# A transformer block on one core: the first token group's evictions, dense groups and norms in another order

## The chip, the cores and the metric

The kernel runs on one core of a Trainium2 chip. A core has five engines with instruction queues of their own: TensorE (PE; it loads weights and multiplies into the accumulator banks of PSUM), VectorE (DVE), ScalarE (ACT), GpSimd (POOL) and SyncE (SP, which here issues every DMA). Each queue runs strictly in order, and engines wait for each other on semaphores. The metric is the time of one execution on the device in microseconds. Three runs of the kernel before took 260.52 us in the median (260.51 to 261.05).

## The reference

One adaptive-norm transformer block over 2048 tokens of 512 features, in bfloat16. A vector `c` gives six rows of modulation; then an attention in a sliding window of 256 keys with 32 heads of 16, and then an MLP across the tokens:

```python
mod = (_silu(c) @ w_mod).reshape(c.shape[0], 6, 1, -1)      # sa, ca, ga, sb, cb, gb
h = _layernorm(x) * (1 + ca) + sa
qkv = (h @ wqkv)                                            # 32 heads of 16
scores = q k^T * 16 ** -0.5, masked to 0 <= i - j < 256
x = x + ga * ((softmax(scores) @ v) @ wo)
h = _layernorm(x) * (1 + cb) + sb
u = gelu(einsum('bsd,sf->bdf', _layernorm(h), w1) + b1)     # sums over tokens
x = x + gb * (einsum('bdf,fs->bds', u, w2) + b2).T
```

## The kernel before

The 2048 tokens are four token groups of 512 (`tg` 0 to 3), each of four tiles of 128. The attention works through units `u`: in a token group, four groups of eight heads (`g8`), and in each of these five kinds `k`, so 20 units per token group, with the place `ul = 5 * g8 + k`. A unit has score products on PE (into two tiles `pss` of a pool of three, each of two banks), two exponentials on ACT (`et`, L614, halves a = 0 and 1), and products with V (into `po`, the one bank of the attention's products). Kinds 0 and 1 are the even heads, kind 2 is the far corner of the window for both, kinds 3 and 4 are the odd heads. In token group 0, kinds 0 and 3 have four score products with narrow exponentials (512 columns), kinds 1 and 4 twelve with wide ones (1024), kind 2 thirty-two with wide ones.

All else on PE is a dense group: 16 products of 512 columns, or 8 transpositions, into the single bank `dn`, which VectorE evicts before the next may begin. Dense groups are V of a tile (`v_group`, L283), q or k of eight heads (`qk_group`, L306), the transpositions of the normed tokens (`transpose_group`, L252), the modulation rows (`bc_group`, L336, which reads eight loads of `wmod` and sends its result through DRAM into `bc`), the biases (`bias_group`, L359) and wo. One unit takes at most one dense group.

The order is written out by the program itself. In the loop from L912, unit u issues: the first exponential, the scores of unit u + 1, then (if unit u - 1 is of kind 2 or 4) the products of u - 1, the dense group, the second exponential, the eviction of the group, and otherwise only now the products of u - 1. `plan` (L778) says with `lay(ul, group)` at which place of the token group each dense group stands. Groups of the next token group (its first q, k and two V tiles, its transpositions) are laid into the end of the one before. Before unit 0 there are V of tile 0 (through `po`) and of tile 1 (through `dn`).

Work of VectorE and GpSimd that isn't bound to a place stands in chains: lists of steps with costs. `fill` puts a step into VectorE's queue where the planner's own clocks (`clock`, in us) say that the engine has time; a chain whose step gave GpSimd work goes on only when the planner's clock of GpSimd says so. The first norm of the next token group is such a chain: statistics on VectorE (`ln1_stats`, L228), for every second tile a reciprocal root on GpSimd, and `ln1_apply` (L240), which for later token groups is 2 GpSimd instructions per tile. GpSimd also makes the even and odd copies of q (L330) and the quotient of the attention (`merge`, L683). `fold_wod` (L826) multiplies wo by a row of `bc`, also on GpSimd.

SyncE's queue in token group 0, in order, after the first inputs: at unit 0 two copies of V (`copy_vc`, L649, of tiles 0 and 1 into `Vc`), then a load of x, two fills of `Vc` with zeros, and x, `wmod`, `wo` in pieces "paced" behind exponentials, with two more copies of V each at units 3, 4 and 5. The copies of a group of heads are read by the products of its kinds 2 and 4.

After unit 79 the MLP follows, with TensorE alone as its tight engine.

Of the kernel before, what the change touches and what calls it, by code (L numbers as in the profile page):

```python
# [20 lines left out]
ND = D // P  # L21
# [9 lines left out]
def kernel(  # L31
# [327 lines left out]
    def bias_group(pool):  # L359
        def mms():  # L360
            pb = pool.tile([P, NF + NT], DT.bfloat16, name="dn")
            nc.tensor.transpose(pb[:], b12[:], identity[0 : NF + NT, 0 : NF + NT])
            return pb

        def evac(pb):
            nc.vector.tensor_copy(out=bFM[:], in_=pb[:])
        return mms, evac, 0.2
# [37 lines left out]
    with tc.manual_schedule():  # L405
# [372 lines left out]
        def plan(tg):  # L778
            at, then = {}, {}

            def lay(ul, group):
                assert ul not in at, (tg, ul)
                at[ul] = group

            def qk(ul, g, g8, kind):
                lay(ul, qk_group(g, g8, kind, ps_dn))

            for n in (2, 3):
                lay(n - 2, v_group(tg, n, ps_dn))
            if tg == 0:  # L790
                for ul, g8, kind in ((2, 1, "q"), (3, 1, "k"), (4, 2, "q"), (5, 2, "k"), (6, 3, "q"), (7, 3, "k")):
                    qk(ul, tg, g8, kind)
                lay(8, bias_group(ps_dn))
                lay(13, bc_group(ps_dn))
                then[18] = [(lambda g=g: fold_wod(g), 0.0) for g in range(ND)]
            else:
                if tg == 1:
                    order = ((2, 1, "k"), (3, 2, "q"), (4, 2, "k"), (5, 3, "q"), (8, 3, "k"))
                else:
                    order = ((2, 2, "k"), (3, 3, "q"), (4, 3, "k"))  # L800
                for ul, g8, kind in order:
                    qk(ul, tg, g8, kind)
                for ul, fc, k in {2: ((8, 10, 0), (10, 11, 0)), 3: ((8, 13, 0), (10, 12, 0), (11, 12, 1))}.get(tg, ()):
                    lay(ul, part_group(fc, k))
                for ul in (6, 7, 9, 10) if tg == 1 else (5, 6, 7, 9):
                    tb = next(wo_next)
                    lay(ul, wo_group(tb, ps_dn))
                    then[ul] = ln23(tb)
            if tg + 1 < NG:
                t0, t1, q0, v0, k0, q1, v1 = (10, 11, 12, 16, 14, 15, 18) if tg == 0 else (11, 12, 13, 14, 15, 17, 16)  # L810
                lay(t0, transpose_group(tg + 1, 0, ps_dn))
                lay(t1, transpose_group(tg + 1, 1, ps_dn))
                lay(v0, v_group(tg + 1, 0, ps_dn))
                lay(v1, v_group(tg + 1, 1, ps_dn))
                for ul, g8, kind in ((q0, 0, "q"), (k0, 0, "k"), (q1, 1, "q")):
                    qk(ul, tg + 1, g8, kind)
                if tg:
                    qk(18, tg + 1, 1, "k")
                    qk(19, tg + 1, 2, "q")
            else:  # L820
                for n, fc in enumerate((6, 7, 8, 9)):
                    for k in range(2):
                        lay(12 + 2 * n + k, part_group(fc, k))
            return at, then
# [6 lines left out]
        def at_unit(tg, ul, u, behind):  # L831
            if ul == 0 and tg + 1 < NG:
                st = lambda g, t0=0: [
                    (lambda tl=tl: ln1_stats(g, tl), 0.8, lambda tl=tl: 4 * g + tl in loaded) for tl in range(t0, 4)
                ]

                def ap(tl):
                    ln1_apply(tg + 1, tl)
                    return 1.13
                add_chain((st(1) if tg == 0 else []) + [(lambda tl=tl: ap(tl), 0.0) for tl in range(4)], first=True)  # L840
                if tg == 0:
                    add_chain(st(2) + st(3))
            if tg == 0 and ul == 6:
                nc.vector.memset(mod_add[:], 0.0)
                nc.vector.memset(mod_add[32:64, :], 1.0)
                nc.vector.tensor_copy(out=sT_rep[:], in_=sT[:].unsqueeze(2).to_broadcast([P, ND, 32]))
                clock["dve"] += 0.42
            if tg == 0 and ul % 5 == 3:
                ones_of_v(1, ul // 5, ul // 5 + 1)
                clock["act"] += 0.5  # L850
            if tg == 0 and ul == 1:
                for half in range(2):
                    part64 = slice(64 - 64 * half, 128 - 64 * half)
                    dma.dma_start(
                        out=Vc[half][part64, :, 8:H, :],
                        in_=zero[part64, :].rearrange("p (h d) -> p h d", d=2 * DH)
                        .unsqueeze(1).to_broadcast([64, 4, H - 8, 2 * DH]),
                    )
            if tg == 0 and 2 <= ul < 6:
                loaded.update((4 + 2 * ul, 5 + 2 * ul))  # L860
            if ul in (3, 4, 5) or (tg < 2 and ul == 0):
                copies_for(tg, max(ul - 2, 0))
            if 0 < tg < NG - 1 and ul == 17:
                copies_for(tg + 1, 0)
            while q_loads and ul != 3:
                load_q(*q_loads.pop(0))
            if tg == 0 and ul < 4:
                pair = slice(8 + 2 * ul, 10 + 2 * ul)
                paced(xall[:, pair, :], x_rows[:, pair, :], behind)
            if tg == 0 and 2 <= ul < 10:  # L870
                v, js = (2, 4, 3, 5)[ul // 2 - 1], slice(ul % 2 * 2, ul % 2 * 2 + 2)
                paced(wmod[:, js, v * D : (v + 1) * D], w_mod_v[:, js, v * D : (v + 1) * D], behind)
            if tg == 0 and 10 <= ul < 12:
                js = slice(ul % 2 * 2, ul % 2 * 2 + 2)
                paced(wod[:, js, :], wo_v[:, js, :], behind)
            if tg == 1 and ul == 2:
                modw.release()
                w1box["pool"] = tc.alloc_tile_pool(name="w1pool", bufs=1, side="right")
                w1box["a"] = w1box["pool"].tile([P, NA, F], DT.bfloat16, name="w1a")
                w1box["v"] = B_w1.rearrange("(sc p) f -> p sc f", p=P)  # L880
                w1box["sc"] = iter([(sc, n) for sc in range(NA) for n in range(2)])

            for sc, n in [x for x in [next(w1box.get("sc", iter(())), None)] if x]:
                part_f = slice(n * F // 2, (n + 1) * F // 2)
                paced(w1box["a"][:, sc, part_f], w1box["v"][:, sc, part_f], behind)
# [19 lines left out]
                on_pool(for_pool)  # L905

        emit_scores(0)
        mms, evac, _ = v_group(0, 1, ps_dn)
        evac(mms())
        clock.update(pe=1.3, dve=2.4, dn=1.4)  # L910
        ready = {0: (0.5, 0.5)}
        for u, (tg, g8, k) in enumerate(units):  # L912
            ul = 5 * g8 + k
            if ul == 0:
                at, then = plan(tg)
            half = 0.5 if (tg, k) in ((0, 0), (0, 3)) else 0.92
            behind = emit_exp(u, 0)
            before = clock["act"]
            clock["act"] = max(clock["act"], ready[u][0]) + half
            if u + 1 < len(units):  # L920
                emit_scores(u + 1)
                if units[u + 1][2] == 2:
                    first = max(clock["pe"], before) + 0.3
                    clock["pe"] = max(first, clock["act"] + 0.05) + 0.42
                else:
                    first = clock["pe"] = max(clock["pe"], clock["act"] - 0.1) + 0.4
                ready[u + 1] = (first + 0.1, clock["pe"] + 0.1)
            closes = u > 0 and units[u - 1][2] in (2, 4)
            if closes:
                products(u - 1)  # L930
            group = at.get(ul)
            if group:
                tile_ = group[0]()
                clock["pe"] = max(clock["pe"], clock["dn"]) + (0.55 if group[2] > 1 else 0.2 if group[2] == 0.2 else 0.9)
            emit_exp(u, 1)
            clock["act"] = max(clock["act"], ready[u][1]) + half
            if group:
                fill(clock["pe"] + 0.05)
                evacuate(group, tile_)
                if ul in then:  # L940
                    add_chain(then[ul])
            if u > 0 and not closes:
                products(u - 1)
            fill(clock["pe"])
            at_unit(tg, ul, u, behind)
        u += 1
        emit_av(u - 1)
# [206 lines left out]
```

## Time and profile before

| what | value |
| --- | --- |
| median of 3 runs | 260.52 us |
| the profiled execution | 259.97 us, its span 258.2 us |
| PE busy | 238.8 us, 92% of the span |
| ACT busy | 164.7 us, 64% (nearly all of it before 166 us) |
| DVE busy | 171.3 us, 66% |
| POOL busy | 120.7 us, 47% |
| attention, token group 0 | 13.9 to about 50 us |
| MLP | from about 166 us to the end |

A line of a timeline gives the start and length in us, the engine and line, what is written and read, and how many such instructions are merged; in brackets the idle time of the engine just before and what ended it. Line numbers are those of the kernel before.

### The profile page before, as it was taken

What the parts mean: (1) busy time and instruction counts of PE and PEld (TensorE: products, weight loads), DVE (VectorE), ACT (ScalarE), POOL (GpSimd) and SP (SyncE); (2) the same over time, 40 slices, a digit from 0 to 9 for tenths busy, and PEclk for the clock granted to TensorE, in tenths of its full rate; (3) what the DMA queues carried; (4) which work ended last, traced back from release to release, by engine and by line L of the source; (5) the groups of instructions that cost most, each with busy time, mean ns of one, the idle gap of its engine ahead of it and who ended that gap; (6) DMA issues with size and microseconds to landing.
All of it is one profiled execution on the core that took longest, in us unless ns stands there. A gap on an engine that the chain in (4) does not pass through costs nothing.

```text
span 258.2 us, 11273 instructions
## 1 busy us (share of the span) xinstructions
PE 238.8 (92%) x4993; PEld 129.5 (50%) x4993; DVE 171.3 (66%) x361; ACT 164.7 (64%) x193; POOL 120.7 (47%) x206
## 2 busy tenths in 40 slices
PE   6988879899989999999999999999999999999994
PEld 2534445455555565555555555544444444444444
DVE  6678878875788888888777897589703112432454
ACT  6588998999999999999999999500055220000000
POOL 6103963689367998887655699664300000000000
PEclk9999999999999999999999999999999999999999
DMA  6949781236630433110103200699960000202031
GB/s 171 332 137 250 219 277 60 62 84 166 189 112 13 147 95 81 37 43 20 38 25 91 60 6 4 205 396 419 420 273 1 0 0 3 81 0 81 20 104 41
DMA packets 27333, 30.76 MB, mean 119 GB/s; under 512 B 3988, under 2 KB 24468, under 8 KB 27284
## 3 DMA queue, kind: packets, MB, share of 16 engines
q1 hardware_dynamic: 27284, 30.04, 36.0%
q8 instruction: 39, 0.64, 1.0%
q14 instruction: 10, 0.08, 0.1%
HBM read 22.55 MB, written 2.23 MB: 96 GB/s over the span
## 4 chain that ended last, share of the span: by engine, by line
PE 70%; DVE 22%; issue 3%; ACT 3%; POOL 0%; DVEq 0%; ACTq 0%; POOLq 0%
PE dn L278 19%; PE py L1117 19%; PE pu L995 8%; PE pu L1081 6%; DVE t L671 4%; PE pss L564 4%; DVE VaugT L294 3%; PE po L625 3%; PE po L639 3%; ACT et L614 3%; DVE qs L323 2%; PE pss L433 2%; DVE KT L320 2%; DVE x L387 2%; DVE ln_stats L699 2%
## 5 line engine op out<-in xcount | busy, mean ns | idle before, releaser
L614 ACT ACTIVATE et<-pss 128x1024 bf16<-128x1024 f32 (+1 forms) x160 | 144.2, 987 | 5.7 <-PE pss L571 5.0
L1117 PE MATMUL py<-guT,w2r 128*128 128x512 bf16 (+1 forms) x238 | 48.5, 366 | 0.0
L278 PE MATMUL dn<-h1T,wqkv 128*32 128x512 bf16 x496 | 33.0, 380 | 4.5 <-DVE qs L323 1.0
L1117 PEld LDWEIGHTS <-w2r 128*128 128x128 bf16 x238 | 23.3, 98 | 25.3
L1096 DVE SCALAR_TENSOR_TENSOR o<-py,bFM,bc 128x512 bf16<-128x512 f32 (+1 forms) x17 | 11.7, 715 | 29.5 <-PE py L1117 29.5
L564 PE MATMUL pss<-QT,KT 32*128 32x64 bf16 (+2 forms) x704 | 27.3, 237 | 3.4 <-ACT et L614 2.1
L671 DVE STREAM_TRANSPOSE t<-po 128x512 f32<-128x512 f32 x32 | 22.7, 709 | 9.2 <-PE po L639 9.1
L211 POOL TENSOR_SCALAR ln_ve<-ln_mv 128x1 f32<-128x1 f32 (+1 forms) x38 | 9.0, 238 | 39.7 <-DVE ln_mv L233 17.9
L215 POOL TENSOR_TENSOR ln_rstd<-ln_ve,mhalf 128x1 f32<-128x1 f32 (+1 forms) x40 | 24.2, 605 | 5.7 <-DVE ln_ve L211 2.6
L625 PE MATMUL po<-et,VaugT 128*32 128x64 bf16 (+2 forms) x704 | 25.0, 240 | 0.0
L564 PEld LDWEIGHTS <-KT 32*128 32x128 bf16 x704 | 14.7, 92 | 18.2 <-issue 8.9
L625 PEld LDWEIGHTS <-VaugT 128*32 128x32 bf16 x704 | 17.8, 96 | 10.4 <-issue 0.5
L278 PEld LDWEIGHTS <-wqkv 128*32 128x32 bf16 x512 | 13.4, 95 | 14.0 <-issue 6.2
L683 POOL TENSOR_TENSOR merge<-t,zr 128x512 bf16<-128x512 f32 x16 | 16.9, 1057 | 3.5 <-DVE zr L682 3.5
L571 PE MATMUL pss<-mask_q,mask_k 32*128 32x256 bf16 (+1 forms) x256 | 18.5, 261 | 0.0
L278 PE MATMUL dn<-wqkv,h1T 128*32 128x512 bf16 x240 | 15.7, 380 | 2.2 <-DVE VaugT L294 0.9
L1006 ACT ACT_TABLE_LOAD x1 | 1.3, 1283 | 24.6 <-issue 24.6
L715 POOL TENSOR_TENSOR h<-h,bc 128x512 bf16<-128x512 bf16 x12 | 13.9, 1156 | 5.3 <-DVE h L711 5.3
L1004 DVE TENSOR_TENSOR gelu_a<-pu,part 128x512 f32<-128x512 f32 x8 | 5.2, 687 | 16.3 <-PE pu L1081 16.3
L278 PE MATMUL dn<-wod,OTd 128*32 128x512 bf16 x192 | 12.6, 381 | 2.1 <-DVE part L772 0.8
L716 POOL TENSOR_TENSOR h<-h,bc 128x512 bf16<-128x512 bf16 x12 | 13.9, 1160 | 0.9
L1081 PE MATMUL pu<-hb,w1b 128*128 128x512 bf16 x64 | 14.3, 379 | 0.0
(113 smaller groups left out, 366.8 us busy)
## 6 DMA issues: line engine op xcount, KB each, us to landing
w2r<-in_B_w_dram SPq DMA_DIRECT2D x14, 512.0 KB, 9.7
w1a<-in_B_w_dram SPq DMA_DIRECT2D x16, 224.0 KB, 3.0
w1b<-in_B_w_dram SPq DMA_DIRECT2D x8, 448.0 KB, 5.9
Vc<-VaugT SPq DMA_DIRECT2D x32, 64.0 KB, 2.4
wmod<-in_w_mod_dram SPq DMA_DIRECT2D x8, 256.0 KB, 4.5
out_dram<-otile SPq DMA_DIRECT2D x15, 128.0 KB, 1.7
x<-in_A_x_dram SPq DMA_DIRECT2D x6, 256.0 KB, 5.7
Vc<-VaugT SPq DMA_DIRECT2D x12, 128.0 KB, 3.1
```

Source lines behind the costliest of these rows:

```text
L215: nc.gpsimd.tensor_tensor(out=r[:], in0=ve[:], in1=mhalf[:, 0:n], op=ALU.pow)
L278: nc.tensor.matmul(out[cols, :], lhsT=lhsT[:, cols], rhs=rhs, start=start, stop=stop, tile_position=(0, 32 * j), skip_group_check=True,)
L564: nc.tensor.matmul(pss[j // 2][:, j % 2, c0 : c0 + nq], lhsT=keys(kb, g8)[rows[j], k0 : k0 + P], rhs=QT[tg][g8][rows[j], par, q0 : q0 + nq ...
L571: nc.tensor.matmul(pss[j // 2][:, j % 2, :].rearrange("p (a r) -> p a r", a=2)[:, 0:n, :] .rearrange("p a (b q) -> p a b q", q=64)[:, :, 0 ...
L614: act = nc.scalar.activation(out=et[:, :, 0:n], in_=state.pop((u, a))[:, :, 0:n], func=ACT.Exp, scale=SCORE_SCALE,)
L625: nc.tensor.matmul(state["po"][32 * j : 32 * j + 32, q0 : q0 + nq], lhsT=VaugT[kb // 4][:, kb % 4, 8 * g8 + 2 * j + par, :], rhs=state["e" ...
L671: nc.vector.transpose(out=state["t2"][:, par, :], in_=state["po"][:])
L683: nc.gpsimd.tensor_tensor(out=m[:].rearrange("p (b a d) -> p a b d", a=2, d=DH), in0=t2v[:, :, :, 0:DH], in1=zr[:].to_broadcast([P, 2, 16, ...
L715: nc.gpsimd.tensor_tensor(out=h2[:], in0=h2[:], in1=bc_cb1, op=ALU.mult)
L995: nc.tensor.matmul(pu[:, i, :], lhsT=w1_of(sc, fc), rhs=hb[sc][:], start=(sc == 0), stop=(sc == NT - 1),)
L1081: nc.tensor.matmul(pu[:, i, :], lhsT=w1_of(sc, fc), rhs=hb[sc][:], start=(sc == s0), stop=(sc == NT - 1),)
L1117: nc.tensor.matmul(pys[n][:, 0 : hi - lo], lhsT=w2r[:, fc, tb * P : (tb + 1) * P], rhs=guT[fc][:, lo:hi], start=(fc == 0), stop=(fc == NF ...
```

## The change

It concerns token group 0 alone. V of tile 2 takes the place ahead of unit 0 through `dn`, and V of tile 1 goes to place 0 through `po`, the bank of the attention's products; the planner's clock of `dn` isn't moved by that. The dense groups get new places: before, 0 to 8 without a gap, then 10 to 16 and 18; after, places 5, 10 and 15 are empty (bias 8 to 13, bc 13 to 12, the transpositions 10 and 11 to 9 and 11, the next group's q 12 to 14, k 14 to 16, V 16 and 18 to 17 and 18, second q 15 to 19). The fold of wo starts one place earlier. The first norm of token group 1 is applied on GpSimd in pairs of tiles: two statistics, two applications, two statistics, two applications, where before all four statistics came first.

```diff
-            for n in (2, 3):
-                lay(n - 2, v_group(tg, n, ps_dn))
+            lay(0, v_group(tg, 2, ps_dn) if tg else v_group(tg, 1, ps_po, "po"))
+            lay(1, v_group(tg, 3, ps_dn))
             if tg == 0:
-                for ul, g8, kind in ((2, 1, "q"), (3, 1, "k"), (4, 2, "q"), (5, 2, "k"), (6, 3, "q"), (7, 3, "k")):
+                for ul, g8, kind in ((2, 1, "q"), (3, 1, "k"), (4, 2, "q"), (6, 2, "k"), (7, 3, "q"), (8, 3, "k")):
                     qk(ul, tg, g8, kind)
-                lay(8, bias_group(ps_dn))
-                lay(13, bc_group(ps_dn))
-                then[18] = [(lambda g=g: fold_wod(g), 0.0) for g in range(ND)]
+                lay(13, bias_group(ps_dn))
+                lay(12, bc_group(ps_dn))
+                then[17] = [(lambda g=g: fold_wod(g), 0.0) for g in range(ND)]
...
-                t0, t1, q0, v0, k0, q1, v1 = (10, 11, 12, 16, 14, 15, 18) if tg == 0 else (11, 12, 13, 14, 15, 17, 16)
+                t0, t1, q0, v0, k0, q1, v1 = (9, 11, 14, 17, 16, 19, 18) if tg == 0 else (11, 12, 13, 14, 15, 17, 16)
...
-                def ap(tl):
-                    ln1_apply(tg + 1, tl)
-                    return 1.13
-                add_chain((st(1) if tg == 0 else []) + [(lambda tl=tl: ap(tl), 0.0) for tl in range(4)], first=True)
+                def ap(*tls):
+                    for tl in tls:
+                        ln1_apply(tg + 1, tl)
+                    return 1.13 * len(tls)
+                if tg == 0:
+                    steps = st(1)
+                    for n in (2, 0):
+                        steps.insert(n + 2, (lambda n=n: ap(n, n + 1), 0.0))
+                else:
+                    steps = [(lambda tl=tl: ap(tl), 0.0) for tl in range(4)]
+                add_chain(steps, first=True)
...
-        mms, evac, _ = v_group(0, 1, ps_dn)
+        mms, evac, _ = v_group(0, 2, ps_dn)
...
+                free = clock["dn"]
                 evacuate(group, tile_)
+                if u == 0:
+                    clock["dn"] = free
```

## The prediction

> **What bounds the kernel now.** I read the page's parts 4 and 5, then the ScalarE, TensorE and SyncE timelines from 12 to 62 us, then DMA by stretch. The page first:
>
> ```profile
> L614 ACT ACTIVATE et<-pss 128x1024 bf16<-128x1024 f32 (+1 forms) x160 | 144.2, 987 | 5.7 <-PE pss L571 5.0
> PE 70%; DVE 22%; issue 3%; ACT 3%; POOL 0%; DVEq 0%; ACTq 0%; POOLq 0%
> ```
>
> The chain runs through PE, yet from 14 to 165 us ScalarE is the tighter engine: 144.2 us of exponentials, 5.0 idle waiting for score masks. Where the idle lies, by the ScalarE timeline:
>
> ```profile
> 15.34 4.90 ACT L614 ACTIVATE et<-pss 128x1024 bf16<-128x1024 f32 x6 [0.33 <-PE pss L571]
> 21.14 1.94 ACT L614 ACTIVATE et<-pss 128x1024 bf16<-128x1024 f32 x2 [0.39 <-PE pss L571]
> 23.45 1.08 ACT L614 ACTIVATE et<-pss 128x512 bf16<-128x512 f32 x2 [0.38 <-PE pss L571]
> 24.98 4.82 ACT L614 ACTIVATE et<-pss 128x1024 bf16<-128x1024 f32 x6 [0.44 <-PE pss L571]
> 30.84 7.74 ACT L614 ACTIVATE et<-pss 128x1024 bf16<-128x1024 f32 x10 [0.53 <-PE pss L571]
> 39.61 2.92 ACT L614 ACTIVATE et<-pss 128x1024 bf16<-128x1024 f32 x4 [0.52 <-PE pss L571]
> 43.24 4.82 ACT L614 ACTIVATE et<-pss 128x1024 bf16<-128x1024 f32 x6 [0.71 <-PE pss L571]
> 48.44 14.24 ACT L614 ACTIVATE et<-pss 128x1024 bf16<-128x1024 f32 x15
> ```
>
> Seven holes, 3.3 us, all in group 0; after 48.44 the gaps sum to 1.2 us. So whatever moves the first exponential of unit 19 (48.44) moves the end, and 3.3 us is all there is. A wide exponential follows the last by 0.947 (15 in 14.24), a narrow one by 0.50 to 0.54.
>
> The TensorE rows show why: one bank, dn, for all dense groups.
>
> ```profile
> 15.65 1.05 PE L278 MATMUL dn<-wqkv,h1T 128*32 128x512 bf16 x16 [0.36 <-DVE VaugT L294]
> 23.01 0.29 PE L564 MATMUL pss<-QT,KT 32*128 32x256 bf16 x4 [0.80 <-DVE KT L320]
> 39.65 1.05 PE L342 MATMUL dn<-wmod,sT_rep 128*32 128x512 bf16 x16
> ```
>
> A turn of dn is 1.05 products, 0.70 eviction, two handovers of 0.04: 1.85 us. And the queue that the change touches unseen, SyncE with its engines' load:
>
> ```profile
> 15.66 1.35 SPq L649 DMA_DIRECT2D Vc<-VaugT  x2
> 17.11 0.54 SPq L425 DMA_DIRECT2D x<-in_A_x_dram  x1
> 31.23 1.96 SPq L425 DMA_DIRECT2D wmod<-in_w_mod_dram  x4
> ```
> ```profile
> 26.00:29.50 3.50, 2.84 (x88) 1.50 (x84) 2.45 (x7) 3.50 (x6) 3.23 (x6) 1.00 0.90 255
> 30.60:32.10 1.50, 0.91 (x42) 0.53 (x33) 1.48 (x4) 1.26 (x2) 1.50 (x3) 1.00 0.40 104
> 34.00:37.40 3.40, 2.72 (x104) 1.77 (x92) 2.53 (x6) 3.40 (x4) 2.37 (x4) 1.00 0.97 308
> ```
>
> (The last two columns are DMA share and GB/s.) SyncE issues without a pause from 15.66 to 33.70; what comes late at its head is late throughout. The last wmod load is issued at 32.77 and lands 4.6 later, at 37.37; its reader at 39.65 doesn't notice.
>
> **The change, part by part.** I walk each queue in its new order with these durations: an eviction starts 0.04 after the last product, dn is free 0.04 after its end, a unit's exponential starts 0.60 after its 12-product scores start (0.44 for 4), and a unit's second score tile waits for the first exponential of the unit before it.
>
> *V1 in po, V2 first.* Removes the dn wait of 0.36 before the second V group and 0.41 before q1. V1's products run at 15.23 (po is free at 14.71), V3 at 16.67 instead of 17.49, q1 at 18.59 instead of 19.33, k1's eviction ends at 22.21 instead of 22.95, so unit 5's exponential starts at 22.71 instead of 23.45: -0.74. It adds a wait: unit 0's products need po back at 17.05; PE reaches them at 17.53, free. But V1's eviction is now third on VectorE, 16.32 to 17.01 instead of 14.91 to 15.60, and the first SyncE copies read V1: 17.07 instead of 15.66. Behind them stand all loads, +1.41. The copies land 2.1 after issue in the trace (17.76, 18.48), so at 19.17 and 19.89; unit 2's products want them at 20.23: 0.3 to spare.
>
> *Dense places, first half.* Unit 5 has no dense group; k2, q3, k3 are one unit later. VectorE takes two statistics of group 2 (0.80 each) ahead of k2's and q3's evictions, since the planner thinks it free; evictions then start at 26.92 and 29.2, 0.3 and 0.5 after their products end. Unit 9's exponential starts at 29.51 instead of 30.84 (-1.33), but k3, then the transposes at unit 9, queue for dn, and unit 11's starts at 33.1 to 33.5 instead of 33.74: -0.2 to -0.6. The upper end is where unit 7's products wait for the second set of copies, which landed at 28.75 (PE is there at 29.28, before it was 30.67).
>
> *First norm in pairs.* Same instructions on GpSimd, but two of 1.13 stand before the odd q mask of g8 = 1: ready at 23.7 instead of 22.14. Its reader, unit 7's scores, comes at 24.48 instead of 26.20. Costs nothing with 0.8 us of cover; without it, the lateness. The second pair ends at 29.1; the transposes come at 31.7 or later. The row of the sT_rep copy (29.13, 0.71 us for 128x128, while GpSimd's merge ran 28.70 to 29.76) against 0.22 for the 64x256 copy says VectorE copies can stall beside GpSimd: the even q mask on VectorE at 20.40 now meets the pair, at worst +0.6 on unit 5, absorbed by bc's wait below.
> [...]
>
> *bc one unit earlier.* This is the dear step. PE comes to it at 36.2 to 36.6 instead of 39.65. It reads all eight wmod loads; the last feeds its twelfth product of 16. Landing of that load, L: at best 37.37 (no delay carried), at worst by SyncE alone 38.78 (all 1.41 carried). DMA shares of 0.90 to 0.97 make the delay stick, but the stretch 30.60 to 32.10 at 0.40 holds 0.9 us of idle that a later, denser stream fills: 1.41 - 0.9 = 0.5 carried, 37.9. To that comes an instruction block: q8's 39 packets of 16 KB take 1.06 us each on one DMA engine; the one at 36.07 falls on the next load (wod), whose last sixteenth lands at 39.15, the fifteenth at 38.05. PE will be over 1 us further by then, so the block falls on the wmod loads: 0 to 1.1. I count 0.4, as the part in reach is the end of one load: L = 38.3. Then 0.27 for the last products, 0.34 for unit 11's, 0.60 to the exponential of unit 14: 39.51 instead of 39.61, -0.1. Behind the waiting bc stand those products and unit 14's scores, so ScalarE idles 0.7 to 1.1 there (it is free at 38.4 to 38.8).
> bc's own DMAs (one write, four reads) go about 2 us earlier into a SyncE that is idle from 35.25 to 41.52; the fold behind them may hold GpSimd 0.7, whose next needed result is at unit 25. Nothing. The bias transposition (0.17) moves to a cover of 1 us. Nothing.
>
> *Dense places, second half.* Unit 15 is empty. ScalarE then needs 6 wide, 4 narrow and one ones_of_v (0.52 to the next): 5.68 + 2.00 + 0.52 = 8.20 from unit 14 to unit 19, where it took 8.83: -0.63. q0', k0', V0', V1', q1' now at 14, 16 to 19 take turns of 1.85 on dn; unit 19's scores are ready 0.13 before ScalarE, so I charge 0.13.
>
> Sum: -0.10 - 0.63 + 0.13 = -0.6. The profiled execution took 259.97 (span 258.2 and 1.77 around it), so 259.37; the runs' median is 260.52, 0.2% above it: 259.9. In general the end moves by L - 38.9.
>
> **The rivals.**
> The whole delay sticks: L from 38.5 to 39.4, at 38.78 -0.1: 260.4. For it: SyncE solid for 18 us, DMA at 0.9 or more. Against: the 0.40 stretch, and that one engine of 16 is behind (x issued at 17.11: fifteen parts by 19.78, the last at 22.32, with a block at 19.66), which a later start may spare.
> [...]
> Slower: bc waits longer still. Full delay and a whole block, 38.78 + 1.1 = 39.9, and the end moves +1.0: 261.5. It decides from L = 39.4. For it: the block is sure to come, only its place is open. Against: the last loads' sixteen parts now land within 1.4 us of each other.
> The loads come in time, L = 37.4: ScalarE alone sets unit 14, end -1.5, 259.0. Against: nothing of the delay may be carried, and no block hit.
>
> **How the numbers follow.** A change under 0.2% (0.52 us) can't be told from none here. Forecast (L 37.6 to 38.5, 259.2 to 260.1) 0.45, of it 0.38 beyond the bound; in time 0.10: faster 0.48. Full delay 0.22: same 0.29. Later still, with it the thin covers (0.13, 0.3) failing: slower 0.23. The range goes down to 258.9 and up to 261.4.
>
> **What would show it.** First copies on SyncE at about 17.1; PE idle of 1 to 2 us inside bc at 36 to 38.5, released by a wmod load; unit 5's exponential near 22.7, unit 14's near 39.5, unit 19's near 47.8; no hole at unit 16. Wrong if bc doesn't wait, if unit 2's or 7's products wait for copies by over 1 us, or if new holes appear after unit 19.

## The result, and the profile after

The change made the kernel slower: 263.26 us in the median of 22 runs (260.72 to 265.21) against 260.26 us in 22 runs of the kernel before (259.37 to 262.06). The ratio is 1.0081, with a 95% interval from 1.0052 to 1.0109. (It leaves out the runs far above the fastest of their kernel, so it is smaller than the ratio of the medians.) The forecast was 259.9 us, with a range up to 261.4.

The profiled execution of the changed kernel took 264.1 us, with a span of 262.4. Its first exponential starts at 14.56, where before it was 13.92. That 0.64 us lies in the first loads, ahead of anything the change touches, and the other profiles below scatter from 13.6 to 14.4. So I subtract 0.64 from times of this profile where I compare them with the forecast, and call them aligned. From the start of the first exponential to the end of the last, the attention took 154.84 us (151.34 before): 3.50 of the 4.13 us between the two profiled executions lie there, the rest is the 0.64.

The exponentials (L614) in the ScalarE timeline of the changed kernel, in the columns of the forecast's fences:

```profile
15.98 4.75 ACT L614 ACTIVATE et<-pss 128x1024 bf16<-128x1024 f32 x6 [0.33 <-PE pss L571]
21.27 1.94 ACT L614 ACTIVATE et<-pss 128x1024 bf16<-128x1024 f32 x2
23.59 1.09 ACT L614 ACTIVATE et<-pss 128x512 bf16<-128x512 f32 x2 [0.39 <-PE pss L571]
25.12 4.75 ACT L614 ACTIVATE et<-pss 128x1024 bf16<-128x1024 f32 x6 [0.44 <-PE pss L571]
30.41 2.93 ACT L614 ACTIVATE et<-pss 128x1024 bf16<-128x1024 f32 x4
34.05 4.75 ACT L614 ACTIVATE et<-pss 128x1024 bf16<-128x1024 f32 x6 [0.71 <-PE pss L571]
42.78 2.92 ACT L614 ACTIVATE et<-pss 128x1024 bf16<-128x1024 f32 x4 [3.47 <-PE pss L571]
47.25 4.75 ACT L614 ACTIVATE et<-pss 128x1024 bf16<-128x1024 f32 x6 [1.55 <-PE pss L571]
52.55 7.44 ACT L614 ACTIVATE et<-pss 128x1024 bf16<-128x1024 f32 x8
```

Up to the row at 34.05 the attention runs ahead of the kernel before: unit 9's exponential (30.41, aligned 29.77) comes 1.07 us earlier. Then there are two large holes: 3.47 us ahead of unit 14 and 1.55 us ahead of unit 16, where the kernel before has 0.52 and 0.71. The TensorE timeline shows what PE did meanwhile:

```profile
36.97 0.33 PE L571 MATMUL pss<-mask_q,mask_k 32*128 32x128 bf16 x4
37.40 0.39 PE L342 MATMUL dn<-wmod,sT_rep 128*32 128x512 bf16 x2
38.17 0.58 PE L342 MATMUL dn<-wmod,sT_rep 128*32 128x512 bf16 x1 [0.38 <-DMA wmod<-in_w_mod_dram]
39.64 1.87 PE L342 MATMUL dn<-wmod,sT_rep 128*32 128x512 bf16 x13 [0.88 <-DMA wmod<-in_w_mod_dram]
40.89 1.03 PE L625 MATMUL po<-et,VaugT 128*32 128x256 bf16 x12
...
44.29 1.90 PE L278 MATMUL dn<-h1T,wqkv 128*32 128x512 bf16 x16
...
48.90 1.05 PE L278 MATMUL dn<-h1T,wqkv 128*32 128x512 bf16 x16
```

bc (L342) starts at 37.40, does two products, and waits twice for loads of `wmod`: 0.38 us for the fifth of the eight, 0.88 us for the seventh. (The eighth landed at 40.30, and its first reader, the twelfth product, ran at 40.45 without a wait.) All the while the products of unit 11 and the scores of unit 14 stand behind it. And then something that the forecast does not have at all: the sixteen dense products at 44.29 take 1.90 us, where sixteen of the same form take 1.05 us at 48.90. The stretches show why. (Columns: busy time and count of each engine, then the granted TensorE clock, DMA share, GB/s.)

```profile
34.75:38.16 3.41, 2.63 (x51) 1.16 (x42) 2.48 (x5) 3.41 (x6) 1.06 (x1) 1.00 0.97 301
38.16:41.58 3.42, 2.53 (x25) 1.21 (x25) 0.04 (x1) 1.15 (x3) 0.00 (x0) 0.50 0.64 218
41.58:44.99 3.41, 3.03 (x60) 1.43 (x62) 2.28 (x5) 2.21 (x3) 0.00 (x0) 0.50 0.11 38
44.99:48.41 3.42, 3.42 (x93) 1.94 (x89) 1.80 (x4) 1.87 (x4) 1.38 (x3) 0.50 0.50 153
48.41:51.82 3.41, 3.16 (x86) 1.66 (x79) 2.79 (x6) 3.41 (x5) 3.01 (x4) 1.00 0.03 7
```

TensorE's clock is granted in full up to 38.16, at half from there for 10.24 us, three steps of 3.41, and in full again from 48.41. In the profile before it is in full until the last microsecond. The page has the same in two digits, and the chain of its part 4 now runs through DMA:

```profile
PEclk9999995899999999999999999999999999999999
...
PE 69%; DVE 18%; DMA 7%; issue 2%; ACT 2%; SPq 1%; DVEq 0%
```

The steps of the runs without a profile are an estimate from their mean granted clock: in the profiled executions one step of 3.41 us at half goes with a mean of 0.993 (e12 below), two with 0.987 (e14), three with 0.980 (the changed kernel). Of the 22 runs of the changed kernel 6 had no such step and took 261.01 us in the mean, 4 had one (261.53), 6 had two (263.80), 6 had three (264.49). The kernel before has them too, but seldom more than one: of 76 runs in the later comparisons, 46 had none, 29 had one. In the 36 of the first of these comparisons 22 without took 259.85 us and 13 with one took 260.49. So the change costs about 1.2 us where the clock holds (261.01 against 259.85), and 4 to 5 us where it falls for two or three steps. These are differences between two comparisons, whose runs of the kernel before have medians of 260.26 and 260.01, so they may be off by some 0.3 us.

### The profile page after: what moved, and what is told of

Its sections match the earlier page's. It is cut to its first block, busy times and chain, and to the rows that moved or that the text cites. A ratio compares the mean times of both kernels' runs of the same rounds, so it can differ in the third digit from the quotient of the medians.

```text
span 262.4 us, 11273 instructions
## 1 busy us (share of the span) xinstructions
PE 243.5 (93%) x4993; PEld 131.1 (50%) x4993; DVE 171.8 (65%) x361; ACT 164.6 (63%) x193; POOL 120.8 (46%) x206
## 4 chain that ended last, share of the span: by engine, by line
PE 69%; DVE 18%; DMA 7%; issue 2%; ACT 2%; SPq 1%; DVEq 0%
PE dn L278 19%; PE py L1127 18%; PE pu L1005 8%; PE pu L1091 6%; DMA wmod<-in_w_mod_dram 4%; PE pss L564 4%; PE po L625 3%; PE po L639 3%; DVE t L671 3%; DVE VaugT L294 3%; DVE qs L323 2%; DMA Vc<-VaugT 2%; ACT et L614 2%; DVE x L387 2%; DVE KT L320 2%
## 5 line engine op out<-in xcount | busy, mean ns | idle before, releaser
L614 ACT ACTIVATE et<-pss 128x1024 bf16<-128x1024 f32 (+1 forms) x160 | 143.9, 988 | 9.4 <-PE pss L571 8.6
L278 PE MATMUL dn<-h1T,wqkv 128*32 128x512 bf16 x496 | 33.9, 388 | 3.5 <-DVE VaugT L294 1.1
L625 PE MATMUL po<-et,VaugT 128*32 128x64 bf16 (+2 forms) x704 | 26.0, 245 | 0.0
L625 PEld LDWEIGHTS <-VaugT 128*32 128x32 bf16 x704 | 18.5, 98 | 10.9 <-issue 0.8
L564 PEld LDWEIGHTS <-KT 32*128 32x128 bf16 x704 | 14.4, 93 | 16.1 <-issue 6.0
L278 PE MATMUL dn<-wqkv,h1T 128*32 128x512 bf16 x224 | 14.7, 381 | 1.7 <-DVE qs L323 0.7
```

What stands on the lines that cost most here:

```text
L278: nc.tensor.matmul(out[cols, :], lhsT=lhsT[:, cols], rhs=rhs, start=start, stop=stop, tile_position=(0, 32 * j), skip_group_check=True,)
L564: nc.tensor.matmul(pss[j // 2][:, j % 2, c0 : c0 + nq], lhsT=keys(kb, g8)[rows[j], k0 : k0 + P], rhs=QT[tg][g8][rows[j], par, q0 : q0 + nq ...
L614: act = nc.scalar.activation(out=et[:, :, 0:n], in_=state.pop((u, a))[:, :, 0:n], func=ACT.Exp, scale=SCORE_SCALE,)
L625: nc.tensor.matmul(state["po"][32 * j : 32 * j + 32, q0 : q0 + nq], lhsT=VaugT[kb // 4][:, kb % 4, 8 * g8 + 2 * j + par, :], rhs=state["e" ...
```

## The experiments

All ratios are against the kernel before, run on the same chip. "ACT part" is the time in the profile from the start of the first exponential to the end of the last; it is free of the scatter in the first loads, but it is that of one run: the run profiled of e9 lies 0.83 us below e9's median and has a part 0.54 shorter than before, though e9's median is no lower. Differences of half a microsecond between these parts decide nothing. "Steps" is the number of half-clock steps in that profile, and in how many runs there was at least one.

| kernel | median, us | ratio [95%] | ACT part, us | steps; runs with any |
| --- | --- | --- | --- | --- |
| before | 260.26 | | 151.34 | 0 |
| after | 263.26 | 1.0081 [1.0052, 1.0109] | 154.84 | 3; 16 of 22 |
| e3: ten products ahead of bc | 261.27 | 1.005 [1.003, 1.007] | 152.70 | 0; 0 of 12 |
| e1: x behind wmod | 260.33 | 1.0003 [0.9969, 1.0037] | 150.20 | 0; 6 of 12 |
| e2: bc at 13 | 259.93 | 0.9996 [0.9968, 1.0024] | 151.56 | 0; 4 of 12 |
| e8: x behind wmod, zeros first | 258.47 | 0.993 [0.9914, 0.9947] | 149.78 | 0; 1 of 12 |
| e4: before, bc at 12 | 260.56 | 1.0023 [1.0003, 1.0042] | 152.39 | 1; 9 of 12 |
| e5: V1 through po alone | 260.31 | 1.0004 [0.9981, 1.0027] | 151.14 | 0; 6 of 12 |
| e9: before, e8's moves | 260.58 | 1.0018 [0.9997, 1.0039] | 150.80 | 0; 4 of 12 |
| e11: before, zeros twice | 263.87 | 1.0141 [1.0122, 1.016] | 154.55 | 2; 5 of 5 |
| e12: e5 with e8's moves | 260.34 | 1.0022 [1.0003, 1.004] | 151.51 | 1; 5 of 6 |
| e13: e8 with V1 as before | 259.17 | 0.9973 [0.9953, 0.9993] | 149.93 | 0; 0 of 6 |
| e14: e8 without the pairs | 262.59 | 1.0102 [1.0083, 1.012] | 154.14 | 2; 4 of 5 |

### What is the wait, and what is the clock: ten products ahead of bc (e3)

The added products multiply zeros into bc's own bank, and bc overwrites them. They need no load, so PE works where it would wait.

```diff
             ps_b = pool.tile([P, D], DT.float32, name="dn")
+            for i in range(10):
+                nc.tensor.matmul(ps_b[:], lhsT=identity[:], rhs=zero[:, 0:D], start=True, stop=True)
```

> The changed kernel with ten idle products of 128x512 (0.22 us each, 2.2 us) on dn ahead of bc's own, in the time in which PE waits. A with the clock as its larger part: the wait stays, its end is set by the load, but PE isn't idle and the clock stays up: all runs like the undisturbed ones of the changed kernel, 0.6 to 1.2 us above the kernel before (ratio 1.002 to 1.005), none 3 us above. If the half clock were not caused by the wait: runs of 3 us above remain, ratio 1.008 or, with the added products on the path, up to 1.016.

Measured: 261.27 us, none of 12 runs with a half-clock step. The TensorE timeline of this kernel (its lines lie two further down):

```profile
37.47 2.33 PE L341 MATMUL dn<-zero,identity 128*128 128x512 bf16 x9
39.73 1.05 PE L344 MATMUL dn<-wmod,sT_rep 128*32 128x512 bf16 x16
```

bc begins 25.69 us after the first exponential (in the changed kernel its seventh load was there at 25.08), waits for nothing, and its 16 products take 1.05 us. The ACT part is 152.70: 1.36 above before, and 2.14 below after. So with the clock held the change leaves the kernel at most 1.36 us behind (up to 0.6 of it may be the ten products, which end later than the seventh load landed), and the half clock adds 2.1 us or a little more. The 1.36 is net of what the change gains; against the same kernel with its loads in time (e8 below, 149.78) it is 2.92. That the clock holds when products fill this stretch is shown by this pair. That the wait as such lets it fall is not: the ten products also add work, and in e4 and e12 below it falls with no wait in bc. Nor did the wait of 0.88 us begin the fall: in the changed kernel's profile the clock falls at 38.16, when only the wait of 0.38 is over.

### What makes the load late: the queue (e1, e8, e9)

In e1 three of the four loads of x that stand between the first copies and the `wmod` loads go behind them. In e8 the two fills of `Vc` with zeros go ahead of the first copies too, into the time in which SyncE waits for V1's eviction (6.4 us in the changed kernel's profile; the first pair of lines below, which e1 does not have).

```diff
-            if tg == 0 and ul == 1:
+            if tg == 0 and ul == 0:
...
-            if tg == 0 and ul < 4:
-                pair = slice(8 + 2 * ul, 10 + 2 * ul)
-                paced(xall[:, pair, :], x_rows[:, pair, :], behind)
+            if tg == 0 and ul == 0:
+                paced(xall[:, 8:10, :], x_rows[:, 8:10, :], behind)
...
+            if tg == 0 and 9 <= ul < 12:
+                pair = slice(2 * ul - 8, 2 * ul - 6)
+                paced(xall[:, pair, :], x_rows[:, pair, :], behind)
```

> The changed kernel, with the three loads of x for tiles 10 to 15 moved behind the eight wmod loads in SyncE's queue; nothing else. Theory A (the loss is bc waiting for the last wmod load, and the half clock that follows): 768 KB less stand before that load, about 3 us at 255 GB/s, so it lands near 36.7 after the changed kernel's own start, PE doesn't wait, no stretch at half clock, and the end is 1.0 to 1.5 us before the kernel before: ratio 0.994 to 0.996. Theory B (the new places and VectorE order themselves cost, the wait only stands in for them): the time stays 0.8 us or more above the kernel before, ratio 1.003 to 1.010.

> The changed kernel with the three loads of x moved behind the wmod loads and also the two zero fills of Vc ahead of the first copies of V (they go in time in which SyncE waits for V1); nothing else. A: 1.5 MB less stand between the copies and the last wmod load, which lands 2 us or more before bc is reached (at about 36.8 from the changed kernel's start): no wait in bc, the undisturbed runs at 258.3 to 259.0, 0.9 to 1.5 us below the undisturbed ones of the kernel before, half clock at most as often as there (14 of 36 runs). B: no better than with the x loads moved alone (undisturbed runs at 259.1), half clock in half of the runs.

> The kernel before with the same two moves in SyncE's queue, as a control. A: its bc doesn't wait, so earlier loads bring nothing: ratio 0.998 to 1.002. If the loads held more than bc: faster by 0.5 us or more, and the gain of the run beside it isn't the change's.

Counted from the first exponential, the last `wmod` load is issued at 18.85 before, 20.53 after, 18.77 in e1 and 17.23 in e8. e1 missed its expectation: 1.76 us earlier was too little, because it only restores the old time of issue, and PE comes to bc 3.1 us earlier than before (22.63 against 25.73). In its profile bc still waits:

```profile
36.47 0.83 PE L342 MATMUL dn<-wmod,sT_rep 128*32 128x512 bf16 x11
37.83 0.59 PE L342 MATMUL dn<-wmod,sT_rep 128*32 128x512 bf16 x5 [0.54 <-DMA wmod<-in_w_mod_dram]
```

Here it is the twelfth product that waits, as the forecast had it, and half of the runs still have half-clock steps: 259.09 us in the mean without, 261.07 to 263.91 with. In e8 nothing waits:

```profile
37.25 1.05 PE L342 MATMUL dn<-wmod,sT_rep 128*32 128x512 bf16 x16
```
```profile
33.90 4.75 ACT L614 ACTIVATE et<-pss 128x1024 bf16<-128x1024 f32 x6 [0.42 <-PE pss L571]
38.48 0.68 ACT L417 ACTIVATE VaugT<-ones 128x512 bf16<-128x512 bf16 x1
39.05 7.79 ACT L614 ACTIVATE et<-pss 128x1024 bf16<-128x1024 f32 x10
46.67 0.68 ACT L417 ACTIVATE VaugT<-ones 128x512 bf16<-128x512 bf16 x1
47.38 9.46 ACT L614 ACTIVATE et<-pss 128x1024 bf16<-128x1024 f32 x10
```

The two holes are gone, and from unit 14 to unit 19 ScalarE takes 8.32 us (24.67 to 32.99 from the first exponential) where it took 8.83: -0.51, and the forecast's terms for this piece were -0.63 + 0.13. e8 is the fastest kernel of the study, 0.7% below the kernel before. The same two moves in the kernel before (e9) gain nothing in the runs (1.0018), where bc does not wait for its loads. So what the changed kernel lost, it lost because its loads came after their reader, with the half clock that followed.

### The reader's place (e2, e4)

e2 is the changed kernel with bc and the biases exchanged (bc at 13, biases at 12). e4 is the kernel before with bc at 12 and the next group's q at 13.

```diff
-                lay(13, bias_group(ps_dn))
-                lay(12, bc_group(ps_dn))
+                lay(12, bias_group(ps_dn))
+                lay(13, bc_group(ps_dn))
```

> The changed kernel with bc back at place 13 and the biases at 12. A: PE comes to bc 1.3 to 1.9 us later and the load at the same time, so 1 us of wait is left; half clock in fewer runs, end between 0.3 us before and 1.5 us after the kernel before (ratio 0.999 to 1.006). B: as the changed kernel, ratio 1.008.

> The kernel before with bc at place 12 and the next group's q at 13, nothing else. A: the last wmod load lands at 37.4 there, PE comes at 37.8, so no wait: within 0.3 us of the kernel before (ratio 0.998 to 1.002). The early place alone is then not the cause, but it together with the late loads. If the place alone were: 1 us or more above, ratio over 1.004.

e2 took 259.93 us, no different from before: the wait in bc is still there (its fourth product starts 1.05 us after its third), as bc comes to PE only 1.9 us later than in the changed kernel, and 1.0 before its old time. Place 13 takes back the loss, but the gain of e8 stays out. In e4 bc comes at 24.93 after the first exponential, its loads are in time, and it does not wait; the 3 runs without a half-clock step took 260.01 us (before: 259.85). The other 9 had one step and took 260.97. So a bc one place earlier is harmless in itself when its loads are there and the clock holds, but in these runs this order met the half clock more often (9 of 12, against 14 of 36 before), with no wait in bc.

### Late loads in the old order (e11)

The kernel before, with its fills of zeros issued twice: 768 KB more on the queue ahead of most `wmod` loads.

```diff
-                for half in range(2):
+                for half in (0, 1, 0, 1):
```

> The kernel before with the two zero fills of Vc issued twice, 768 KB more ahead of the wmod loads and no other change: the suspected cause alone, put into the old order. A: the last wmod load lands 2.5 to 3 us later, at about 40, bc (reached at 39.65) waits 0.4 to 1 us: 0.3 to 1.0 us slower in undisturbed runs, half clock in more runs than before, the kernel as a whole 1.002 to 1.008. If late loads don't matter: ratio 0.999 to 1.001.

Measured: 263.87 us. But the profile shows another reader than the one meant. The last `wmod` load is issued 5.6 us later than before, and bc does not wait. The second copies of V are late, and unit 7's products wait:

```profile
33.59 0.52 PE L639 MATMUL po<-et,Vc 128*32 128x64 bf16 x24 [2.59 <-DMA Vc<-VaugT]
...
43.10 1.05 PE L342 MATMUL dn<-wmod,sT_rep 128*32 128x512 bf16 x16
```

So it supports the order of things (a late transfer on SyncE's queue, a wait of PE, two half-clock steps by the profile's mean clock of 0.987, 3.2 us in the ACT part; the 24 products with `Vc` take 0.52 us at the end of that wait and 0.36 at 42.89), and says nothing on the loads of `wmod` themselves.

### The parts of the change (e5, e12, e13, e14)

e5 is the kernel before with V1 through po and V2 first, nothing else. e12 is e5 with e8's two moves. e13 is e8 with V1 through dn ahead of unit 0 as before. e14 is e8 with the first norm as before (four statistics first), and so the first transpositions at place 10. The core of e14:

```diff
-                if tg == 0:
-                    steps = st(1)
-                    for n in (2, 0):
-                        steps.insert(n + 2, (lambda n=n: ap(n, n + 1), 0.0))
-                else:
-                    steps = [(lambda tl=tl: ap(tl), 0.0) for tl in range(4)]
+                steps = (st(1) if tg == 0 else []) + [(lambda tl=tl: ap(tl), 0.0) for tl in range(4)]
...
-                t0, t1, q0, v0, k0, q1, v1 = (9, 11, 14, 17, 16, 19, 18) if tg == 0 else (11, 12, 13, 14, 15, 17, 16)
+                t0, t1, q0, v0, k0, q1, v1 = (10, 11, 14, 17, 16, 19, 18) if tg == 0 else (11, 12, 13, 14, 15, 17, 16)
```

> The kernel before with V1 through po and V2 first, alone; the dense groups at their old places, the norm as before. A: the copies go out 1.4 later, as in the changed kernel, the last wmod load lands 2 us later, PE reaches bc at place 13 at 38.5 to 39 and waits up to 1 us, so the gain of 0.7 at the start is mostly given back: ratio 0.998 to 1.002 in undisturbed runs, half clock somewhat more often. If V1 through po costs by itself: unit 5's exponential isn't earlier, ratio over 1.003.

> The kernel before with V1 through po and the two moves in SyncE's queue (the fills with zeros ahead of the first copies, three loads of x behind wmod); the dense places and the norm as before. Theory A (the moves give the loads back in time, so V1's gain at unit 5 is no longer taken by bc, but the old order has later holes at units 7 to 16 that swallow most of it): 259.8 to 260.4, ratio 0.998 to 1.001, bc without a wait. Rival B (what bank V1 takes is the whole gain of the version with all parts and the moves, which took 258.47): 258.5 to 259.0, ratio 0.993 to 0.996.

> The changed kernel with the two moves in SyncE's queue, and V1 and V2 as in the kernel before (V1 through dn ahead of unit 0, V2 at place 0 through dn); the dense places and the pairs stay. Theory A (the new places carry most of the gain, unit 5 loses 0.74 again, of which half is absorbed by later holes): 258.6 to 259.2, ratio 0.994 to 0.997, first copies near 1.75 after the first exponential. Rival B (the gain is V1's): 260.2 to 260.6, ratio 1.000 to 1.002.

> The changed kernel with the two moves in SyncE's queue, the first norm applied after all four statistics as in the kernel before, and so the first transpositions at place 10 instead of 9 (at 9 the normed tokens would not be there). Theory A (the pairs cost nothing and gain nothing but the place 9): within 0.5 of 258.47, so 258.4 to 259.0, ratio 0.993 to 0.996. Rival C (the pairs delay the even and odd copies of q and cost time): 257.8 to 258.2, ratio 0.990 to 0.992, and the hole ahead of unit 5 or 7 gets smaller by 0.2 or more.

e5 and e12: V1's bank alone gains nothing, with late loads or without (e12, at 1.0022, lies just above the range it was given). Unit 5's exponential is 0.3 us earlier in e5 and 0.4 in e12 (9.22 and 9.15 from the first exponential, 9.53 before), and the old order has lost it again by unit 19 (34.87 and 34.92, 34.52 before). In e12, 5 of 6 runs have a half-clock step; the one without took 259.33 us. e13 kept part of the gain: 0.9973, just beyond its range, with an interval (0.9953 to 0.9993) that does not meet e8's (0.9914 to 0.9947). (The medians of e8 and e13 come from two comparisons whose runs of the kernel before differ by 0.55 us; the ratios are each against its own.) By the runs the new places, with the pairs and the moves, carry some 0.3 of e8's 0.7%, and V1's bank, which gains nothing in the old order, the rest. The profiles do not show that split: e13's ACT part is 149.93, only 0.15 more than e8's. But e13's profiled run was the fastest of its six, and e8's lay 0.4 us above e8's median.

e14 missed both expectations. It took 262.59 us, because at place 10 the normed tokens are not there:

```profile
34.49 0.34 PE L260 MATMUL dn<-identity,xn 128*128 128x128 bf16 x3
36.45 0.45 PE L260 MATMUL dn<-identity,xn 128*128 128x128 bf16 x5 [1.61 <-POOL xn L222]
```

The fourth tile's norm ends on GpSimd at 36.4. The place of the transpositions can only be had with the pairs; they are no part that can be left out. What the pairs cost by themselves is therefore not shown. PE's wait is again followed by half clock, two steps from 37.24 on.

## Why the prediction was wrong

**The copies of V and SyncE's head: right.** The first copies go out at 17.73, aligned 17.09 (forecast 17.07); unit 2's products do not wait.

**Unit 5 and the first half of the places: nearly right.** Unit 5's exponential starts at aligned 22.95 (22.71 forecast, 23.45 before), unit 9's at 29.77 (29.51), unit 11's at 33.41 (33.1 to 33.5). Unit 7's products wait 0.28 us for the second copies, the case that the forecast named as the upper end. The chain of waits passes through that copy, so this is where the delay is first on the path.

**The pairs: right as a cost, incomplete as a part.** No run has them alone; they delay nothing that shows in the profile after, but the forecast priced only their harm. e14 shows what they are for.

**bc's wait: right in kind.** PE comes to bc at aligned 36.76 (forecast 36.2 to 36.6), stops inside it for 0.38 and 0.88 us, and a `wmod` load releases it. The forecast had the twelfth product wait for the last load; it was the third and the fourth product that waited for the fifth and seventh, and the last load held nothing.

**L: the step that failed first.** The forecast let 0.9 of the 1.41 us of delay be absorbed ("a later, denser stream fills") and counted 0.4 us of an instruction block: L = 38.3. Measured, nothing was absorbed. Counted from the first exponential, the copies go out 1.42 us later (3.17 against 1.75) and the last `wmod` load 1.68 later (20.53 against 18.85). The block came nearly whole: one of 16 KB was transferred at 35.39 and took 1.12 us, and the last of the sixteen parts of each of the last four loads landed 0.8 to 1.0 us after the fifteenth (before: 0.0 to 0.1). That the block held this part is inferred from the times. The last load landed at 40.30, aligned 39.66, 1.36 us above the forecast: from the first exponential it landed 2.29 later than before (25.74 against 23.45), where the forecast had 0.93. That is the place of the rival "bc waits longer still", which the forecast gave less than one chance in four: it said L = 39.9 and decided from 39.4. Its +1.0 us agrees in size with the runs in which the clock held (+1.2) and with e3 (+1.36 in the ACT part). The mistake was to take idle DMA engines in one stretch (a share of 0.40) as room for a delay of the issuing queue. SyncE's own rows carry the delay; here are the last five issues of `wmod`, before and after:

```profile
30.59 2.60 SPq L425 DMA_DIRECT2D wmod<-in_w_mod_dram  x5
```
```profile
32.89 2.61 SPq L425 DMA_DIRECT2D wmod<-in_w_mod_dram  x5
```

Their pacing does not hold them: the exponential that the last of these loads is placed behind (unit 9's first) ended at 31.43, and the load was issued at 35.09. The chain of waits runs through the late copy of V and then the seventh load:

```profile
25.60 4.94 DMA Vc<-VaugT
...
34.57 5.03 DMA wmod<-in_w_mod_dram
39.59 0.04 issue
39.64 1.68 PE dn L342 x13
```

**From L to unit 14, and unit 16: the step that is missing.** The forecast added 1.21 us from L to the exponential of unit 14, and no hole at unit 16. Measured were 2.48 us (40.30 to 42.78) and a hole of 1.55, as TensorE ran at half clock. By the forecast's own rule (the end moves by L - 38.9) the measured L gives +0.8; the attention took 3.5 longer, and most of what is missing is this term, which the forecast put at nothing. At unit 19 the changed kernel is 3.47 us behind before (37.99 against 34.52 from the first exponential), e3 only 1.30: so about 2.2 us belong to the clock. The forecast read the granted clock as 1.00 in its rows and took it as given. (The terms of the forecast's turn of dn sum to 1.83 us, not 1.85; nothing hangs on it.) The second half of the places was priced rightly (-0.51 in e8 against -0.50), but in the changed kernel it was lost: from unit 14 to unit 19 ScalarE takes 9.77 us there (28.22 to 37.99), 0.94 more than before.

**The case in which the loads come in time** was forecast at 259.0, with the end 1.5 us earlier. e8 made that case: its ACT part is 1.56 us shorter, and its median 258.47.

**What stays open.** What begins a half-clock step. The step ahead of the fall in the changed kernel had PE busy for 2.63 of 3.41 us, while the kernel before passed one with 2.45 (28.66 to 32.07) and one with 2.33 without a fall:

```profile
35.49:38.90 3.41, 2.33 (x52) 1.32 (x48) 2.42 (x6) 3.41 (x6) 1.09 (x2) 1.00 0.72 237
```

Where the steps of its other runs lie, their means do not tell. No run varied PE's work in such a step by itself.

## What to carry to other kernels

When a reader is moved earlier, compare its new time with the landing of its loads under the queue as the change leaves it, and let a delay at the head of a queue that issues without a pause come through whole, unless the trace shows waits of the issuing engine itself; the idle share of the DMA engines is no such wait (here 1.42 us at the first copies of V became 1.68 at the last load, though a stretch had a DMA share of 0.40 before the change). In this case waits of 1.26 us on TensorE left the kernel 1.2 us behind the kernel before where the granted clock held and 4 to 5 where it fell for two or three steps, so the mean clock of each run belongs beside its time, and a hole in PE's work has to be priced with that chance (16 of 22 runs here, none of 12 with products in the hole). If a change fails because its data come late, look first for other issues on the same queue that can go behind them or into its idle time: here two such moves turned a loss of 0.8% into a gain of 0.7%.

## What the runs showed of the hardware

In the changed kernel's trace the granted TensorE clock falls from 1.0 to 0.5 at 38.16 and is back at 1.0 from 48.41: 10.24 us, three times 3.41. In e12 (below) it is at half for one stretch of 3.42 us, in e14 for two, 6.83 us in sum, and no value but 0.5 and 1.0 shows in the stretches read. In these three profiles it came back after the first such stretch in which PE was busy nearly throughout (3.42 of 3.42 us in the changed kernel, 3.38 of 3.42 in e12, 3.41 of 3.42 in e14), and stayed at half after 2.53 of 3.42 and 3.03 of 3.41 (changed kernel) and 2.81 of 3.41 (e14). This is e12, with no wait in bc at all:

```profile
30.32:33.73 3.41, 2.26 (x89) 1.43 (x79) 2.58 (x7) 3.31 (x5) 3.20 (x7) 1.00 0.59 186
33.73:37.15 3.42, 3.38 (x76) 2.28 (x60) 2.08 (x5) 2.84 (x4) 2.01 (x4) 0.50 0.87 269
37.15:40.56 3.41, 2.90 (x92) 1.64 (x92) 2.59 (x5) 2.79 (x5) 0.73 (x2) 1.00 0.32 105
```

There the fall lasts one step. In the changed kernel the wait of 0.88 us lies in the first half-clock step and a wait of 0.38 for ScalarE in the second, and it lasts three; that these waits prolong it is a reading, not a test. In e14 the step ahead of the fall had PE busy for 1.80 us, and the clock came back after one of 3.41:

```profile
33.83:37.24 3.41, 1.80 (x95) 1.33 (x86) 1.92 (x6) 2.10 (x3) 2.12 (x5) 1.00 0.87 269
37.24:40.65 3.41, 2.81 (x47) 1.25 (x35) 2.54 (x6) 2.62 (x4) 1.05 (x1) 0.50 0.36 118
40.65:44.07 3.42, 3.41 (x71) 1.66 (x64) 1.16 (x3) 1.62 (x3) 0.00 (x0) 0.50 0.11 36
44.07:47.48 3.41, 2.98 (x99) 1.67 (x98) 2.91 (x8) 3.29 (x6) 1.80 (x4) 1.00 0.47 145
```

In the step ahead of the fall in the changed kernel (34.75 to 38.16) the longest stretch in which PE had no work was 0.38 us, and PE was without work for 0.78 us in sum.
